# Separate step orders for the last four query groups, and the last output half scaled on ScalarE

## The chip, the cores and the metric

The kernel runs on one core of a Trainium2 chip. The metric is the device time of one execution in microseconds (us). The kernel before took 464.57 us, the median of 4 runs that lie between 464.2 and 465.14.

Engine names as the profile gives them: PE is TensorE's matmul, PEld its weight load, DVE is VectorE, ACT is ScalarE, POOL is GpSimd, and SP is SyncE, whose queue issues the transfers.

## What is computed

For each of 4 batches there are 12544 rows of q, k and v with 128 columns, and 49 agent rows. Two attentions are chained (agents over k and v, then q over agents), and the result goes through a feed-forward layer with three first matrices of which the largest product counts:

```python
agent_v = softmax(scale * agents @ k.T) @ v          # 49 x 128 per batch
x = softmax(scale * q @ agents.T) @ agent_v          # 12544 x 128 per batch
h = np.maximum(np.maximum(x @ w1, x @ w2), x @ w3)   # 768 wide
out = h @ w_out                                      # 50176 x 128, float32
```

## The kernel before, in words

The kernel never forms x. For each batch it multiplies agent_v into the differences w3-w1 and w2-w1 and into w1 @ w_out once, and keeps the result, 49 agents by 1792 columns, twice (in partitions 0 to 48 and 64 to 112) in a tile named G. After that a group of 1024 query rows needs only its exponentials and matmuls with G. Since max(w1, w2, w3) = w1 + max(w2 - w1, max(w3 - w1, 0)), the hidden layer is a relu, a max, and a linear part. The softmax's division comes last: the output is multiplied by the reciprocal of the sum of the exponentials.

The 50176 rows make 49 such groups, numbered 0 to 48. The k and v work of batches 1 to 3 is spread over earlier groups; the last dozen groups have none of it. A group s consists of these steps (the names are used throughout, as u2.48 for step u2 of group 48; f counts six slices of 128 of the 768 hidden columns):

| step | engine, line | work |
|---|---|---|
| s | PE L504 | 2 matmuls: q times agents |
| ex | ACT L510 | exponential, gives e_q |
| sum, rec | PE L518, DVE L524 | 4 small matmuls, then the reciprocals of the sums |
| u0 to u5 | PE L530 | 2 matmuls of 49 rows, on two halves of the array side by side: slice f of the (w3-w1) product |
| a0 to a5 | ACT L545 (a3: L542) | relu of u; a3 writes back into the same PSUM tile |
| v0 to v5 | PE L530 | 2 matmuls: slice f of the (w2-w1) product; v3 adds onto a3's tile |
| x0 to x5 | DVE L555 (x3: ACT L553) | max of v and a, gives r |
| lin0, lin1 | PE L560 | 2 matmuls that open an output half (4 of 8 blocks of 128 rows) with the linear part |
| oc00 to oc05, oc10 to oc15 | PE L569 | 4 matmuls: slice f of r times w_out onto output half 0 or 1 |
| sc0, sc1 | DVE L576 | output half times the reciprocals, PSUM to SBUF |
| store | SP L583 | one transfer of 512 KB to HBM, after sc0 and sc1 |

Three rings of buffers bind the steps: `uv` (3 PSUM pairs of banks, taken by u and v, freed by a, x), `om` (2 PSUM banks, taken by s, the sums' tile, lin0 and lin1; an output half is freed by its sc), and a_sb (3 tiles in SBUF, from a to x).

The order of the work is written out by hand. Each step gets a key, 6 times its group's number plus an entry of a table that `table(s)` at L101 picks (KEY, LATE, BORDER, BEGIN), and `emit` at L125 sorts all steps by key. A step whose needs or whose ring buffer are not yet met by steps already placed is put aside and goes in as soon as they are. So a table's entry only says where a step wants to stand; one far too early means "as soon as it can". The placed list, cut by engine, is each engine's program order, and engines run in order and wait for each other by semaphores. `put` (L588) sets needs: ex needs s; u needs ex; x needs v and a; oc needs its lin and x; sc needs rec and six oc. `out_scale` at L572 is the step sc. Before the change the last groups, like all from 36 on, use LATE.

Of the kernel before, what the change touches and what calls it, by code (L numbers as in the profile page):

```python
# [11 lines left out]
AF = mybir.ActivationFunctionType  # L12
# [4 lines left out]
def kernel(  # L17
# [18 lines left out]
    nc = tc.nc  # L36
    B, N, C = q.shape
    A = agents.shape[1]
    Dff = moe_w1.shape[1]
    scale = 1.0 / math.sqrt(C)  # L40
# [8 lines left out]
    NQ = B * NT // GT  # L49
# [46 lines left out]
        "oc11": 11.381, "oc13": 11.497,  # L96
    }
    PRODUCT_KEYS = (-8.717, -1.818)
    BEHIND = 2.6

    def table(s):  # L101
        if s + 1 in tails:
            return BORDER
        return BEGIN if s in tails and s < SB else KEY if s < SB else LATE
# [14 lines left out]
    def at(key, fn, name=None, needs=(), ring=None, frees=()):  # L119

        ops.append((key, len(ops), fn, name, needs, ring, frees))
# [140 lines left out]
    def k_group(b, t0, n, key, s):  # L264

        d = {}
        early = s is None
        K = None if early else table(s)
        if s == 0:
            key += BEHIND  # L270

# [109 lines left out]
    def k_tail(b, sum_key, keys, s):  # L381
# [46 lines left out]
        if s is not None:  # L428
            at(6.0 * (s - 1) + table(s - 1)["ke"] + 1.51, reduce, ("sum_e", b), [("kx", s - 1)])
            at(sum_key + 0.8, total, ("total", s), [("sum_e", b), ("ho", s)])  # L430
# [20 lines left out]
    def q_group(s):  # L451
# [4 lines left out]
        d = {}  # L456
# [28 lines left out]
        def evacuate():  # L485
# [4 lines left out]
            if not s:  # L490
                nc.scalar.activation(qT[:, :half], d["qT_ps"][:, :half], AF.Copy)  # L491

        K = table(s)
        q_dma = s >= SB or s + 1 in tails

# [76 lines left out]
        def out_scale(o):  # L572
            if "out" not in d:
                d["out"] = work.tile([P, GT, C], FP32, tag="o_sb", bufs=3, name="o_sb")
            j, m = 2 * pairs[o][0], 2 * len(pairs[o])
            nc.vector.tensor_tensor(  # L576
                out=d["out"][:, j:j + m, :],
                in0=d["o", o].rearrange("p (j c) -> p j c", c=C),
                in1=d["r"][:, j:j + m].unsqueeze(2).to_broadcast([P, m, C]), op=ALU.mult)
# [8 lines left out]
        def put(name, fn, *needs, ring=None, frees=()):  # L588
            at(key + K[name] + (BEHIND if s == 0 and name in ("sum", "rec") else 0), fn, (name, s), needs,
               ring, frees)  # L590
# [42 lines left out]
        for o in range(2):  # L633
            put(f"lin{o}", lambda o=o: out_linear(o), ("ex", s), *new_linear, ring="om",
                frees=[(f"sc{o}", s)])
            for f in range(NF):
                put(f"oc{o}{f}", lambda o=o, f=f: out_hidden(o, f), (f"lin{o}", s), (f"x{f}", s))
            put(f"sc{o}", lambda o=o: out_scale(o), ("rec", s),
                *[(f"oc{o}{f}", s) for f in range(NF)], *([("store", s - 3)] if s >= 3 else []))
# [36 lines left out]
    for b in range(1, B):  # L676
        for g in range(NK):
            s = (b - 1) * NT // GT + g
            hosting.add(s)
            k_group(b, g * KT, min(KT, NT - g * KT), 6.0 * s, s)  # L680
    for s, b in tails.items():
        assert s - 1 not in hosting
        k_tail(b, 6.0 * (s - 1) + table(s - 1)["ho"] + 0.001, [6.0 * s + PRODUCT_KEYS[i] for i in range(2)], s - 1)
    for s in range(NQ):
# [35 lines left out]
```

The softmax here doesn't subtract the row's maximum and nothing guards it: scores larger than these inputs give would overflow.

## Time and profile before

| what | value |
|---|---|
| median of 4 runs | 464.57 us |
| profiled execution, its own time | 465.01 us |
| its span, first to last instruction | 463.2 us |
| granted TensorE clock | 0.999 |
| period of one of the last groups (L542 of groups 46 to 48 starts at 433.50, 441.37 and 449.23) | 7.86 us |
| end of the last DVE instruction | 459.19 us |

The span is what the times inside the profile add up to; the execution's own time is 1.81 us longer. Times below are us from the span's start. The share of busy time says little here, because the matmuls' ends are modelled; what is read is which step started right after which other. In the last groups a group's steps overlap with those of its two neighbours, so that one period of 7.86 us holds one of each step, but of different groups.

### The profile page before, as it was taken

The numbers are of one execution on the slowest core, as the hardware profiler recorded it, in microseconds if no ns is written. First come the engines' busy times: TensorE is split into PE (matmuls) and PEld (weight loads), VectorE is DVE, ScalarE is ACT, GpSimd is POOL, SyncE is SP. The second block draws the span as 40 slices with busy tenths as digits, with TensorE's granted clock in tenths as the row PEclk, the third lists the DMA queues.
The fourth block names the chain that finished last, engine by engine and source line by source line (L and its number), as shares of the span: only waits on it lengthen the run. The fifth ranks groups of instructions, "written<-read, shape, count | busy, mean of one in ns | idle before, by whom it ended". The sixth has DMA issues, their size and how long they took to land.

```text
span 463.2 us, 13350 instructions
## 1 busy us (share of the span) xinstructions
PE 438.1 (95%) x5473; PEld 274.3 (59%) x5473; DVE 403.0 (87%) x512; ACT 396.2 (86%) x460; POOL 171.7 (37%) x179
## 2 busy tenths in 40 slices
PE   2597899999999999999999999999999999999995
PEld 2465466666665666666656666666656555555554
DVE  3255899999988999999989999999988999999995
ACT  3365889989899899899999998998999999999991
POOL 2244963553452545536272446353240101000000
PEclk9999999999999999999999999999999999999999
DMA  8999999996999899997998999996766586644122
GB/s 312 409 410 392 409 347 327 347 332 144 309 304 315 286 250 319 326 275 237 299 321 257 284 320 294 292 260 192 173 137 180 141 190 155 173 125 123 61 93 92
DMA packets 81450, 118.26 MB, mean 255 GB/s; under 512 B 55208, under 2 KB 56684, under 8 KB 81388
## 3 DMA queue, kind: packets, MB, share of 16 engines
q1 hardware_dynamic: 81184, 117.30, 83.2%
q8 instruction: 43, 0.70, 0.6%
q14 instruction: 20, 0.16, 0.1%
q10 hardware_dynamic: 203, 0.10, 0.1%
HBM read 78.74 MB, written 25.69 MB: 225 GB/s over the span
## 4 chain that ended last, share of the span: by engine, by line
PE 80%; DMA 8%; DVE 5%; ACT 4%; issue 1%; SPq 0%; POOL 0%; DVEq 0%; ACTq 0%
PE uv_ps L530 34%; PE o_ps L569 29%; PE o_ps L560 6%; DMA st<-in_k_dram 5%; PE m_ps L483 4%; DVE r L555 4%; PE m_ps L504 3%; ACT a_sb L545 2%; DMA st<-in_q_dram 2%; DMA st<-in_v_dram 2%; PE m_ps L323 2%; PE m_ps L312 1%; PE m_ps L518 1%; DVE o_sb L576 1%; ACT e_q L510 0%
## 5 line engine op out<-in xcount | busy, mean ns | idle before, releaser
L555 DVE TENSOR_TENSOR r<-uv_ps,a_sb 128x1024 bf16<-128x1024 f32 x245 | 297.1, 1220 | 14.7 <-PE uv_ps L530 6.5
L545 ACT ACTIVATE a_sb<-uv_ps 128x1024 bf16<-128x1024 f32 x245 | 240.8, 1026 | 14.9 <-PE uv_ps L530 13.6
L530 PE MATMUL uv_ps<-e_q,G 49*128 49x512 bf16 (+3 forms) x1248 | 187.2, 368 | 2.5 <-ACT uv_ps L542 0.7
L569 PE MATMUL o_ps<-wo_bf,r 128*128 128x128 bf16 x2352 | 175.3, 220 | 0.2 <-DVE r L555 0.2
L569 PEld LDWEIGHTS <-r 128*128 128x128 bf16 x2352 | 137.8, 98 | 40.1 <-issue 38.2
L530 PEld LDWEIGHTS <-G 49*128 49x128 bf16 x1248 | 57.7, 93 | 65.3 <-issue 33.3
L342 POOL TENSOR_TENSOR Eacc<-Eacc,e_k 128x441 f32<-128x441 f32 (+1 forms) x30 | 30.5, 1016 | 129.0 <-ACT e_k L317 129.0
L576 DVE TENSOR_TENSOR o_sb<-o_ps,recips 128x512 f32<-128x512 f32 x98 | 67.5, 689 | 9.2 <-PE o_ps L569 6.3
L478 POOL CAST q_bf<-st 128x1024 bf16<-128x1024 f32 x49 | 51.0, 1042 | 60.7 <-DMA qT<-q_bf 59.4
L553 ACT ACTIVATE r<-uv_ps 128x1024 bf16<-128x1024 f32 x49 | 50.2, 1024 | 18.0 <-PE uv_ps L530 17.7
L280 POOL CAST k_bf<-st 128x1152 bf16<-128x1152 f32 (+2 forms) x45 | 50.6, 1124 | 28.0 <-DMA st<-in_k_dram 24.7
L542 ACT ACTIVATE uv_ps<-uv_ps 128x1024 f32<-128x1024 f32 x49 | 49.6, 1012 | 1.6 <-issue 1.3
L560 PE MATMUL o_ps<-G,e_q 128*128 128x256 bf16 x196 | 38.0, 276 | 0.3 <-DVE o_sb L576 0.3
L287 POOL CAST v_bf<-st 128x1152 bf16<-128x1152 f32 (+1 forms) x33 | 37.5, 1136 | 0.6 <-PE m_ps L504 0.3
L510 ACT ACTIVATE e_q<-m_ps 128x512 bf16<-128x512 f32 x49 | 29.8, 608 | 0.5 <-PE m_ps L504 0.5
L300 DVE COPY kT<-uv_ps 128x1152 bf16<-128x1152 bf16 (+1 forms) x15 | 10.7, 713 | 16.8 <-PE uv_ps L294 16.8
L285 ACT ACTIVATE v_bf<-st 128x1152 bf16<-128x1152 f32 (+1 forms) x12 | 12.9, 1072 | 13.7 <-DMA st<-in_v_dram 13.6
L560 PEld LDWEIGHTS <-e_q 128*128 128x128 bf16 x196 | 12.5, 97 | 19.0 <-issue 17.8
L489 DVE COPY qT<-m_ps 128x1024 bf16<-128x1024 bf16 (+1 forms) x33 | 22.2, 673 | 0.8 <-PE m_ps L483 0.8
L483 PEld LDWEIGHTS <-q_bf 128*128 128x128 bf16 x264 | 14.9, 98 | 13.2 <-issue 10.6
L483 PE MATMUL m_ps<-ident,q_bf 128*128 128x128 bf16 x264 | 20.4, 220 | 0.5 <-POOL q_bf L478 0.5
L504 PE MATMUL m_ps<-qT,agT 128*64 128x512 bf16 (+3 forms) x104 | 19.9, 388 | 0.5 <-ACT qT L491 0.5
(71 smaller groups left out, 227.2 us busy)
## 6 DMA issues: line engine op xcount, KB each, us to landing
st<-in_q_dram SPq DMA_DIRECT2D x46, 512.0 KB, 4.9
out_dram<-o_sb SPq DMA_DIRECT2D x46, 512.0 KB, 3.1
st<-in_k_dram SPq DMA_DIRECT2D x40, 576.0 KB, 6.3
st<-in_v_dram SPq DMA_DIRECT2D x40, 576.0 KB, 7.7
st<-in_k_dram SPq DMA_DIRECT2D x3, 512.0 KB, 7.2
st<-in_v_dram SPq DMA_DIRECT2D x3, 512.0 KB, 7.9
wst<-in_moe_w_dram SPq DMA_DIRECT2D x3, 384.0 KB, 10.5
st<-in_q_dram SPq DMA_DIRECT2D x2, 384.0 KB, 4.8
```

Of the source, the lines that this page charges most:

```text
L280: nc.gpsimd.tensor_copy(out=d["kb"][:, :n, :], in_=d["k"][:, :n, :])
L287: nc.gpsimd.tensor_copy(out=d["vb"][:, :n, :], in_=d["v"][:, :n, :])
L478: nc.gpsimd.tensor_copy(out=d["qb"], in_=d["q"])
L483: nc.tensor.transpose(t[:, j * P:(j + 1) * P], d["qb"][:, j, :], ident)
L530: nc.tensor.matmul(t[:, h, j0 * P:j1 * P], G[b][h * H:h * H + A, col + f * P:col + (f + 1) * P], d["e"][h * H:h * H + A, j0 * P:j1 * P], s ...
L542: nc.scalar.activation(u, u, AF.Relu)
L545: nc.scalar.activation(a_sb[f], u, AF.Relu)
L553: nc.scalar.activation(r, v_ps[f], AF.Relu)
L555: nc.vector.tensor_tensor(out=r, in0=v_ps[f], in1=a_sb[f], op=ALU.max)
L560: nc.tensor.matmul(t[:, i * 2 * C:(i + 1) * 2 * C], d["e"][:, jj * P:(jj + 1) * P], G[batch[jj]][:, C1O:C1O + 2 * C], start=(i == 0), stop ...
L569: nc.tensor.matmul(t[:, c:c + C], r_sb[f][:, h, jj * P:(jj + 1) * P], wo_bf[:, f, :], start=False, stop=True, skip_group_check=True)
L576: nc.vector.tensor_tensor(out=d["out"][:, j:j + m, :], in0=d["o", o].rearrange("p (j c) -> p j c", c=C), in1=d["r"][:, j:j + m].unsqueeze( ...
```

## The change

There is a new list LAST of four tables, one each for groups 45 to 48, with a key for each step, and `table(s)` returns these for them. The last group's sc1 is done by four ScalarE instructions of 128x128, one per block of rows with its own column of reciprocals as scale, in place of one DVE instruction of 128x512.

```diff
+    LAST = [
+        {"v3": -164.4181, "x5": -156.2085, "oc14": -101.5261, "sc0": -56.4089, "a4": -33.1221,
...
+        {"a4": -135.5952, "s": -3.6850, "ex": -2.2030, "ho": -1.9346, "u0": -1.3390,
+         "sum": -0.9715, "a0": 0.1977, "rec": 0.3166, "u1": 1.4697, "u2": 3.5883, "v1": 3.7970,
+         "a1": 3.8096, "u3": 3.9647, "a2": 5.0765, "a3": 5.2628, "x1": 6.1940, "v0": 6.2913,
+         "v2": 6.3762, "v3": 6.7820, "x0": 10.4629, "sc1": 11.0558, "x3": 12.8641, "u4": 13.1350,
+         "v4": 13.7666, "x2": 16.1146, "u5": 19.9425, "v5": 20.9765, "sc0": 27.0577,
+         "x4": 27.8299, "oc04": 43.1860, "a5": 44.1320, "oc15": 44.9180, "lin1": 46.2961,
+         "oc13": 49.5958, "oc11": 49.9320, "oc12": 50.9170, "oc10": 55.9318, "oc14": 57.5404,
+         "oc05": 60.1508, "lin0": 70.3912, "oc03": 74.0752, "oc00": 92.6315, "oc01": 97.6449,
+         "x5": 102.3830, "oc02": 107.1067},
+    ]
     BEHIND = 2.6
 
     def table(s):
+        if s >= NQ - len(LAST):
+            return LAST[s - NQ]
         if s + 1 in tails:
             return BORDER
         return BEGIN if s in tails and s < SB else KEY if s < SB else LATE
...
             j, m = 2 * pairs[o][0], 2 * len(pairs[o])
+            if s == NQ - 1 and o == 1:
+
+                for i in range(m):
+                    nc.scalar.activation(d["out"][:, j + i, :], d["o", o][:, i * C:(i + 1) * C], AF.Copy,
+                                         scale=d["r"][:, j + i:j + i + 1])
+                return
             nc.vector.tensor_tensor(
```

What the keys come to, as program order (the steps of the tail; up to v5.47 the orders of PE differ in which slice's oc stands where, where sum stands, and in the places that the prediction names):

```
PE before:  v5.47 u1.48 oc04.46 oc05.46 u2.48 oc03.46 v0.48 u3.48 lin1.47 oc10.47 oc14.47
            v2.48 v3.48 v1.48 oc15.47 oc13.47 oc12.47 oc11.47 u4.48 u5.48 lin0.47 oc02.47 v4.48
            oc01.47 oc00.47 v5.48 oc04.47 oc05.47 oc03.47 lin1.48 oc10.48 oc14.48 oc15.48 oc13.48
            oc12.48 oc11.48 lin0.48 oc02.48 oc01.48 oc00.48 oc04.48 oc05.48 oc03.48
PE after:   v5.47 u1.48 oc03.46 oc05.46 oc00.46 u2.48 v1.48 u3.48 lin1.47 oc15.47 oc10.47 oc12.47
            oc14.47 v0.48 v2.48 v3.48 oc11.47 oc13.47 lin0.47 oc03.47 oc02.47 u4.48 v4.48
            oc00.47 oc05.47 oc01.47 u5.48 v5.48 oc04.47 lin1.48 oc13.48 oc11.48 oc12.48 oc10.48
            oc14.48 lin0.48 oc04.48 oc03.48 oc00.48 oc01.48 oc15.48 oc05.48 oc02.48
DVE before: x4.47 rec.48 x5.47 sc0.46 x0.48 x2.48 x1.48 sc1.47 x4.48 x5.48 sc0.47 sc1.48 sc0.48
DVE after:  x4.47 rec.48 x5.47 sc0.46 x1.48 x0.48 x2.48 sc1.47 x4.48 sc0.47 x5.48 sc0.48
ACT before: a4.47 a5.47 a0.48 a1.48 a2.48 a3.48 x3.48 a4.48 a5.48
ACT after:  a4.47 a5.47 a0.48 a1.48 a2.48 a3.48 x3.48 a4.48 a5.48 sc1.48 (four instructions)
```

The orders of SP and POOL are the same in both.

## The prediction, made before the changed kernel ran

> **What bounds the kernel now.** I read the page first (its chain of waits), then the timeline of each engine over the last 40 us, then the chain over the last 14 us. The page's chain says that the end hangs on PE, not on transfers:
>
> ```profile
> span 463.2 us, 13350 instructions
> PE 80%; DMA 8%; DVE 5%; ACT 4%; issue 1%; SPq 0%; POOL 0%; DVEq 0%; ACTq 0%
> ```
>
> But the last groups run in a loop of PE and DVE. In one period of DVE's timeline the reader is to see three pieces without a gap after a wait for PE:
>
> ```profile
> 442.73 2.35 DVE L555 TENSOR_TENSOR r<-uv_ps,a_sb 128x1024 bf16<-128x1024 f32 x2 [0.22 <-PE uv_ps L530]
> 445.00 0.68 DVE L576 TENSOR_TENSOR o_sb<-o_ps,recips 128x512 f32<-128x512 f32 x1
> 445.64 1.22 DVE L555 TENSOR_TENSOR r<-uv_ps,a_sb 128x1024 bf16<-128x1024 f32 x1
> ```
>
> These are x2.47 and x1.47, sc1.46, x4.47. u1.48 takes x4.47's buffer and starts at 446.91, 0.05 after it. From u1 to the next group's v2, PE never stops: 3.18 us, by the group before (439.05 to 442.23). So the loop is v2 to x2 0.50, x2 and x1 2.27, sc1 0.64, x4 and hand-over 1.27, PE 3.18: 7.86 us, the period. Both engines have slack outside it.
>
> The end is another stage. The chain of the last 5 us:
>
> ```profile
> 454.56 1.23 DVE r L555
> 455.79 0.05 issue
> 455.83 1.07 PE o_ps L569 x16
> 456.90 0.22 PE o_ps L560 x2
> 457.12 1.35 PE o_ps L569 x24
> 458.47 0.02 issue
> 458.50 0.69 DVE o_sb L576
> ```
>
> After x5.48, the last max, PE still has 42 matmuls, and the last scaling follows alone. The sums by stretch show the same (PE's count is the third column, DVE's the fifth); the last is the store:
>
> ```profile
> 449.23:455.78 6.55, 6.24 (x76) 4.10 (x73) 6.36 (x8) 3.98 (x5) 0.00 (x0) 1.00 0.20 80
> 455.78:459.19 3.41, 2.63 (x42) 2.43 (x42) 1.98 (x3) 0.00 (x0) 0.00 (x0) 1.00 0.41 159
> 459.19:463.20 4.01, 0.00 (x0) 0.00 (x0) 0.00 (x0) 0.00 (x0) 0.00 (x0) 0.87 0.33 131
> ```
>
> **Step sizes.** From PE's starts: an oc step (4 matmuls) is 0.225 (six take 1.35), lin 0.23, a u or v step before another 0.215; going from u/v to the full array or back makes a step 0.325 (0.32 to 0.33). DVE, start to next start: x 1.14, sc 0.63; 1.22 and 0.69 to their ends. ACT: a or x3 0.96 to the next, 1.02 to the end. From end to start: v to x on an idle DVE 0.11, u to a 0.04, v3 to x3 0.09, a buffer to PE 0.05, oc to sc 0.04. A u, v or oc step lasts 0.39 from its start to its end.
>
> **Groups 45 to 47: nothing.** No matmul is added. In the stretch from u1 to v2 other slices' oc stand, in the same number, and all their r tiles are ready; the DVE part has the same four steps. So I cost these orders at nothing; the loop covers them. Four edits depend on that cover.
> - u0.45 no longer follows v4.44 directly: oc01.43 stands between. That costs two array switches (0.22), but u0 waited 0.15 there for a4, so v5 is 0.08 later; and u1 after it waits 0.2 for x4. Without that slack the cost would be 0.08.
> - u5.46 moves behind lin0.45 and oc05.45, and waits with v4 for x1.46 (437.22), as v4 did. a5 still finds ACT busy with a4. Zero; without cover two steps, 0.45.
> - rec.45 and rec.46 move behind x5. Their sc0 comes 0.3 after DVE is free. Zero.
> - ex.45, ex.46 and ex.48 move behind x3. Behind ex wait lin0 (for its PSUM bank) and a4. With the trace's numbers of that period: v3.45 ends 427.11, so x3 runs from 427.20, ex from 428.16 and ends 428.76; lin0.44 starts at 428.82. It just fits, as the 0.48 for which ACT idled before a4 now lies before x3. No row shows ex behind x3, so bounds for lin0's delay: 0 (this sum; no gain, as ex was early before), and 0.17 a group (no overlap of x3 and ex, 0.06, and a hand-over as slow as the slowest in the chain, 0.12 ahead of a3.48). I take 0, the sum that uses the rows of this same engine back to back; three times 0.17 is for the range.
>
> **Group 48's order.** I follow the new program order from u1.48 (446.91, still tied to x4.47).
> - PE: oc03, oc05, oc00 of 46; u2.48 at 448.01. v1.48 needs x5.47's buffer (448.21): 448.26. u3 448.48, lin1.47 448.79, four oc, v0 450.02, v2 450.24. v3 needs a3: a2 starts when u2 ends, 448.44, a3 449.40, ends 450.42; v3 450.47. Then oc11, oc13, lin0, oc03, oc02 of 47, u4 452.02, v4 452.24, three oc, u5 453.34, v5 453.56, oc04.47 453.88, lin1.48 454.11.
> - DVE: sc0.46 finds its oc00 done (448.08) and starts at 448.13, not 448.55. x1.48 448.76 to 449.98. x0 has to wait for v0's end (450.41): 450.52; x2 451.66; sc1.47 452.80; x4 needs a4.48, which runs 452.45 to 453.48: 453.55 to 454.77; sc0.47 454.69; x5 455.32 to 456.54.
> - PE again: five oc of half 1 (oc14 at 455.24, after x4), lin0.48 455.46 (sc0.47 frees its bank at 455.37), four oc of half 0 to 456.59. oc15.48 wants 456.59, when x5 has just ended: no wait. oc05, oc02 456.82 and 457.04, ending 457.43.
>
> So PE issues its last step at 457.04, where the trace of before has it at 458.07 (oc03.48): 1.03 earlier. It is made of the stops of before, v3.48's wait for a3 (0.54 after v2 where 0.215 would do: 0.32) and oc15.48's for x5 (0.59 where 0.225 would do: 0.36), and of array switches: 13 from u1.48 on before, 9 after, four at 0.11; together 1.1, less some 0.05 that PE waits anew at v1 and v3. Nearly the whole gain is therefore PE's; the price is that DVE's x0.48 now stops 0.6 for v0.
>
> **The scaling.** sc0.48 on DVE: 457.47 to 458.16. sc1.48 on ACT follows oc15 (ends 456.98). No row shows a 128x128 scaling by a column from PSUM. Near rows, from the groups by shape:
>
> ```profile
> L240 ACT ACTIVATE wall<-o_ps 128x128 bf16<-128x128 f32 x1 | 0.3, 271 | 0.0
> L425 ACT ACTIVATE G<-uv_ps,r_ag 128x1024 bf16<-128x1024 f32 x3 | 3.3, 1115 | 0.0
> L545 ACT ACTIVATE a_sb<-uv_ps 128x1024 bf16<-128x1024 f32 x245 | 240.8, 1026 | 14.9 <-PE uv_ps L530 13.6
> ```
>
> 271 ns for the shape, and 1115 - 1026 = 89 ns for a column as scale: 0.36 each. The instruction behind such a one starts 1.01 after it (138.72, 139.73 in ACT's timeline), an overlap of 0.10. So four take 3 x 0.26 + 0.36 = 1.14; bounds 1.1 and 1.44 (no overlap). I take 1.14, from the row that has a column too: 457.02 to 458.16, beside sc0. The Trainium skill's page "ScalarE: Activation LUTs", section "Rules for kernel authors", gives plain multiplies to VectorE and not to ScalarE, which speaks against this edit. By the rows it is right for one half: 0.69 on DVE against 1.14. Followed here, DVE would do sc1 at 457.02 and sc0 from 457.65 to 458.34; with ScalarE the end is 458.16. The rule loses 0.18 here, only because DVE has the other half to do; at ScalarE's upper bound, 458.46, it would win by 0.12. So this edit is worth about 0.2 at best, not the 0.63 that it takes from DVE.
>
> sc1's first instruction also waits for transfers: its output buffer was last read by group 45's store, issued near 441.4 with 2.6 to 3.2 us to landing. Nothing is queued behind it on ACT, and the store waits for it and sc0. SP and POOL keep their order.
>
> **The sum.** 459.19 becomes 458.16: 1.03 us. The store and the end keep their 4.01 us, as the same 512 KB go after both halves. Span 462.17, execution 465.01 - 1.03 = 463.98. The runs' median lies 0.44 below that execution: 464.57 - 1.03 = 463.5 us. What a measurement of this kernel can tell from no change is about 0.2%, here 0.93 us; the forecast lies just beyond that line.
>
> **Rivals.**
> - The walk holds (chance 0.70): 463.5, own range 463.1 to 464.1.
> - The last group is starved more than the walk has it (0.24). For: x5.48's end and oc15, sc0.47 and lin0.48, a4 and x4 meet within 0.1 us, and any delay ahead of v0.48 goes through five DVE steps to the end. Against: each size is from this trace. With 0.65 lost on this path: 464.2.
> - Slower (0.06): ex behind x3. A delay d of lin0 goes straight into v4, x4 and u1, that is into the loop, in three groups. It cancels the gain at d = 0.34 and makes the kernel slower by 0.2% from d = 0.65; at 0.7 it gives 464.57 - 1.03 + 2.1 = 465.6. Against: the rows bound d at 0.17.
>
> **Numbers.** Range 463.0 to 464.7: it takes in ScalarE's upper bound (+0.3), the three delays of 0.17, the starved case, and below it the spread of the store's landing (2.6 to 3.2); it leaves out the slower case. Faster by over 0.2%: two thirds of the first case and a little of the second, 0.49; within: 0.45; slower: 0.06.
>
> **What would show it.** In the profile after: the period up to group 47 unchanged, u1.48 near 446.9; lin0.44 and lin0.46 without a wait for ex; PE's last step, oc02.48, starting near 457.0 with few gaps; DVE with one wait of about 0.6 before x0.48; four ScalarE rows of about 360 ns, 1.14 in all, ending within 0.2 of sc0.48. It is wrong if u1.48 is later than 447.1, if oc15 waits for x5, or if ScalarE's part is over 1.5 us.

## The result, and the profile after

The changed kernel takes 463.62 us (median of 34 runs, 463.19 to 464.95) against 464.81 for the kernel before (52 runs, 464.20 to 465.91). The ratio is 0.9977 with a 95% interval of 0.9972 to 0.9981: 1.07 us faster (0.88 to 1.30); the two medians lie 1.19 apart. The forecast was 463.5, a gain of 1.03, counted from the 464.57 of the first four runs.

The profiled execution took 463.82 us, with a span of 461.7. Line numbers in its rows are the old ones plus 40, from `out_scale`'s scaling on plus 46; L619 is new. The page hides the change (PE has 81% of its chain where it had 80%): shares of a 462 us span cannot show 1 us. The chain of the last microseconds does (start, length, engine, tile, line, number of instructions):

```profile
454.35 1.12 PE o_ps L609 x20
455.47 0.22 PE o_ps L600 x2
455.69 1.13 PE o_ps L609 x20
456.82 0.02 issue
456.84 0.37 ACT o_sb L619
```

There is no wait for DVE in it any more, and nearly no "issue" (time in which an engine waited for nothing that the profile shows) before the last scaling: PE goes from one step to the next. Before, the same place held a whole max (1.23 us of DVE) and 42 matmuls behind it. DVE's own timeline shows where the last max stands now, and ACT's row the new scaling:

```profile
454.51 0.68 DVE L622 TENSOR_TENSOR o_sb<-o_ps,recips 128x512 f32<-128x512 f32 x1
455.11 1.21 DVE L595 TENSOR_TENSOR r<-uv_ps,a_sb 128x1024 bf16<-128x1024 f32 x1
457.29 0.69 DVE L622 TENSOR_TENSOR o_sb<-o_ps,recips 128x512 f32<-128x512 f32 x1 [0.96 <-PE o_ps L609]
```
```profile
456.84 1.14 ACT L619 ACTIVATE o_sb<-o_ps,recips 128x128 f32<-128x128 f32 x4 [2.19 <-PE o_ps L609]
```

These are sc0.47, x5.48 and sc0.48, and the four instructions of sc1.48. x5.48 now ends at 456.32, 0.54 later than before, and still the last scalings end at 457.98, 1.21 earlier. Both halves end in the same hundredth. Of the 1.21, 0.11 is no part of the change: this trace runs about that much earlier from well before the changed groups on (a3 of group 41 starts at 394.06, before at 394.19; u1.48 at 446.80, before 446.91). From u1.48 to the end of the last scaling it is 11.18 us, before 12.28: 1.10 gained.

The stretches of the end, in the same columns as before (stretch, length, busy time and count of PE, PEld, DVE, ACT, POOL, clock, transfers):

```profile
447.00:455.00 8.00, 8.00 (x103) 5.71 (x102) 7.46 (x8) 6.21 (x7) 0.00 (x0) 1.00 0.18 70
...
458.00:461.70 3.70, 0.00 (x0) 0.00 (x0) 0.00 (x0) 0.00 (x0) 0.00 (x0) 1.00 0.35 142
```

PE is busy 8.00 of 8.00 us. In the stretch where the old trace had 6.24 of 6.55 busy, with 76 matmuls, this one (449.12 to 455.67, 0.11 earlier) has 6.55 of 6.55 and 91 matmuls. The last stretch, store and end, is 3.70 us where before it was 4.01; the prediction had it unchanged.

### The profile page after: what moved, and what is told of

Its sections match the earlier page's. It is cut to its first block, busy times and chain, and to the rows that moved or that the text cites. A ratio compares the mean times of both kernels' runs of the same rounds, so it can differ in the third digit from the quotient of the medians.

```text
span 461.7 us, 13354 instructions
## 1 busy us (share of the span) xinstructions
PE 437.4 (95%) x5473; PEld 274.5 (59%) x5473; DVE 402.2 (87%) x511; ACT 397.2 (86%) x464; POOL 171.5 (37%) x179
## 4 chain that ended last, share of the span: by engine, by line
PE 81%; DMA 8%; DVE 4%; ACT 3%; issue 1%; SPq 0%; POOL 0%; ACTq 0%; DVEq 0%
PE uv_ps L570 34%; PE o_ps L609 30%; PE o_ps L600 6%; DMA st<-in_k_dram 5%; PE m_ps L523 4%; PE m_ps L544 3%; DVE r L595 3%; ACT a_sb L585 2%; DMA st<-in_q_dram 2%; DMA st<-in_v_dram 2%; PE m_ps L363 2%; PE m_ps L352 1%; PE m_ps L558 1%; DVE o_sb L622 0%; ACT e_q L550 0%
```

## The experiments

The same early step lies up to 0.5 us apart in two traces, so places in different kernels are compared after lining them up at a DVE step that both have in the same place (sc0.46 with the new orders, x4.48 with the old).

**The scaling alone.** The four ScalarE instructions of the diff, put into the kernel before.

> The kernel before with only the scaling moved: group 48's sc1 as four ScalarE instructions, old orders. Theory (the gain is PE's, from group 48's order): sc1.48 is not on the path there, since it starts at 456.94 with 1.5 us to spare before sc0.48 at 458.50, so 0.0 us against before (within 0.1). Rival (the gain is the 0.63 us that DVE no longer does): about 0.6 us faster than before.

Measured: ratio 1.0003 (0.9995 to 1.0011), no difference. What DVE no longer does was not on the path.

**The orders alone.** The new tables without the lines in `out_scale`.

> The changed kernel with sc1.48 back on DVE as one instruction: new orders alone. Theory: DVE does sc1 and then sc0 after the last matmuls, 0.63 + 0.69 from oc15's end, so 0.18 us slower than the changed kernel, about 0.9 us faster than before. Rival (the scaling is half of the change): 0.5 us slower than the changed kernel or more.

Measured: 463.44 us, ratio 0.9970 (0.9959 to 0.9982). In time it cannot be told from the full change. In its profile DVE does both scalings at the end,

```profile
456.68 1.29 DVE L616 TENSOR_TENSOR o_sb<-o_ps,recips 128x512 f32<-128x512 f32 x2 [0.52 <-PE o_ps L609]
```

and ends at 457.97, with sc0.46 0.15 earlier than in the changed kernel: lined up 0.14 later than with ScalarE (expected 0.18). So nearly the whole gain is the orders', and the new scaling is worth 0.14 in the trace and too little for the runs to show.

**Two tables of four.** A miss, and an instructive one.

```diff
-        if s >= NQ - len(LAST):
+        if s >= NQ - 2:
```

> The changed kernel with new tables for groups 47 and 48 only; 45 and 46 keep the old one. Three oc steps of group 46 then stand earlier than in the changed kernel, where PE waits for x4. Theory (the loop covers the orders of groups 45 and 46, and v1.48 waits for x5.47 at the same time): the same time as the changed kernel within 0.15 us, about 1.1 us faster than before. Rival (each of the four tables brings a part): half of the gain or less.

Measured: 466.23 us, ratio 1.0033 (1.0022 to 1.0044), slower than before by 1.5 us. The waits from 430 us on (who waited for whom: us in total, times, longest), first of the changed kernel, then of this one:

```profile
DVE r L595 <- PE uv_ps L570: 0.9, 3, 0.5
```
```profile
DVE r L595 <- PE uv_ps L570: 3.2, 5, 1.0
...
ACT e_q L550 <- PE m_ps L544: 1.0, 1, 1.0
```

The keys of neighbouring groups share one scale. With group 47 on its new table and 46 on the old one, s.47 came to stand behind v1.46, 1.0 us later, ex.47 waited for it, and the loop from u1.47 to u1.48 grew from 7.86 to 8.50 us. So this kernel did not test what it was made for; it says that an order in these groups can cost much, not that the new one gains there. The next two do it with explicit lists.

**Old up to u1.48, then new; and new up to u1.48, then old.** Each step that a list names gets its place from the list, all others keep the key of their table:

```diff
+        step = f"{name[0]}.{name[1]}" if isinstance(name, tuple) else None
+        if step in TAIL:
+            key = 1000 + TAIL.index(step)
         ops.append((key, len(ops), fn, name, needs, ring, frees))
```

> The order of before, step for step, up to u1.48, and from u1.48 on the order of the changed kernel, written as an explicit list (the three steps of oc0 of group 46 that stand behind u1.48 are the same number, of the slices that the old order has left); sc1.48 on ScalarE. Theory (the whole gain is made after u1.48): the changed kernel's time within 0.15 us, some 1.1 us faster than before. Rival (the orders of groups 45 to 47 bring part of it): at most 0.7 us faster.

> The counterpart: the order of the changed kernel up to u1.48, and from there the order of before; sc1.48 on ScalarE as in the changed kernel. Theory: the time of before within 0.15 us. Rival (orders of groups 45 to 47 matter): 0.4 us faster or more.

Measured: 463.34 us, ratio 0.9969 (0.9957 to 0.9980), the whole gain, for the first; 464.76 us, ratio 1.0001 (0.9993 to 1.0009), none of it, for the second. The chain of the first has the end of the changed kernel, without a wait (28 matmuls: seven oc steps), then that of the second, which ends as the old kernel's did:

```profile
455.46 1.58 PE o_ps L579 x28
```
```profile
454.75 1.22 DVE r L605
455.98 0.05 issue
456.02 1.07 PE o_ps L619 x16
```

The three tables' work on groups 45 to 47 neither gains nor costs: the runs say so to within 0.4 us, and in the traces the way from a3 of group 41 to a3 of group 48 is 55.04 us in the second kernel (394.38 to 449.42) and in the kernel before (394.19 to 449.23).

**ex behind x3, twelve times.** In the kernel before, in the table LATE:

```diff
-        "s": -4.972, "ex": -4.712,
+        "s": -4.972, "ex": -4.000,
```

> The kernel before with one entry of the late table changed, so that ex stands behind x3 in 12 groups (37 to 48) instead of in none. Each delay d of lin0 would count 12 times. Theory: d is 0 to 0.05, so 0.0 to 0.6 us slower than before, and the period stays within 0.05 of 7.86. Rival (ex behind x3 delays lin0 by the row-based upper bound of 0.17 or more): 2 us slower or more, period 8.03 or more.

Measured: 464.65 us, ratio 0.9992 (0.9984 to 1.0000). ACT's timeline of one period, behind the row of the kernel before that shows its gap:

```profile
428.71 4.90 ACT L545 ACTIVATE a_sb<-uv_ps 128x1024 bf16<-128x1024 f32 x5 [0.48 <-PE uv_ps L530]
```
```profile
419.21 1.02 ACT L553 ACTIVATE r<-uv_ps 128x1024 bf16<-128x1024 f32 x1 [0.55 <-PE uv_ps L530]
420.13 0.59 ACT L510 ACTIVATE e_q<-m_ps 128x512 bf16<-128x512 f32 x1
420.71 4.90 ACT L545 ACTIVATE a_sb<-uv_ps 128x1024 bf16<-128x1024 f32 x5
```

ACT's gap has moved from behind x3 to in front of it, and a4 follows ex at once. The period is 7.86 us (a3 starts at 417.64 and at 425.50), as before, and all twelve groups have ex behind x3. So no delay d shows, and the slower rival falls.

**Four array switches more.** Two entries of the changed tables, oc04 of group 47 and v4 of group 48 (the rest of their lines is left out):

```diff
-         "oc04": 48.8226, ...
+         "oc04": 26.5100, ...
...
-         "v4": 13.7666, ...
+         "v4": 17.0000, ...
```

> The changed kernel with v4.48 put behind oc00.47 and v5.48 behind oc04.47, so that PE changes between the 49-row steps and the full array four times more and no step's need becomes late. Theory (after u1.48 PE never waits and a switch costs 0.11 us): 0.44 us slower than the changed kernel, PE's last step at 457.3 where the changed kernel has it at 456.86. Rival (the end hangs on DVE's chain to x5.48, PE has slack): no slower, since x5 does not move.

Measured: 464.08 us, ratio 0.9987 (0.9981 to 0.9994), 0.46 slower than the changed kernel, by the two ratios. Its chain:

```profile
451.81 0.32 PE uv_ps L570 x2
452.14 0.33 PE o_ps L609 x4
452.47 0.32 PE uv_ps L570 x2
452.79 0.55 PE o_ps L609 x8
```

Each step that stands alone between two of the other kind is 0.32 to 0.33 instead of 0.22. x5.48 moved by nothing (454.98 to 456.19 with the origin 0.13 earlier), and the end came 0.42 later: PE sets it, and a switch costs about 0.11 (0.42 / 4).

**The last max's matmuls earlier.** In the changed table of group 48, oc15 gets the key 49.7 and x5 49.69, so that x5's matmuls come early while DVE's order stays.

> The changed kernel with oc15.48 moved up to the second oc of its half, with oc05 third in its own half; x5.48 stays where it is on DVE. Theory (the place of the matmuls that need the last max decides the end): PE stops at oc15 until x5 ends at about 456.3, then has 11 steps of 0.22 left, ends its last step's start near 458.8: about 1.9 us slower than the changed kernel, 0.9 slower than before. Rival (the gain came from fewer array switches alone): within 0.2 us of the changed kernel.

Measured: 465.32 us, ratio 1.0017 (1.0010 to 1.0023): 0.8 slower than before (0.9 expected), with all the saved switches in it. The chain shows the old picture, and behind these lines come 26 matmuls more (24 of half 0's and lin0's two) and sc0 from 458.88:

```profile
454.72 1.23 DVE r L595
455.95 0.05 issue
456.00 1.29 PE o_ps L609 x20
```

**One step of the old order moved.** In the old order oc15.48 goes behind oc11.48.

> The kernel before with one step moved: oc15.48, the first step that waits for x5.48, stands behind oc13, oc12 and oc11 of its half instead of ahead of them. Theory (oc15's wait of 0.36 us for x5 is one of the three parts of the gain and can be had alone): 0.3 us faster than before, since PE fills the wait and lin0.48 is then met by its bank's release at 456.4. Rival (DVE's chain sets the end): no change.

Measured: 464.37 us, ratio 0.9993 (0.9984 to 1.0001): not settled by time. In the trace the last scaling ends at 458.76, with x4.48 0.11 earlier: 0.32 gained of the 0.30 expected, and the wait is gone (24 matmuls in one piece):

```profile
455.06 1.34 PE o_ps L576 x24
456.40 0.29 PE o_ps L567 x2
```

**A version meant to be faster.** Since PE has no gap left from u1.48 on, the place to look is what follows its last step. The edits are named in the expectation; the core is a store for each half:

```diff
-        at(key + 12.2, store, ("store", s), [("sc0", s), ("sc1", s)])
+        if s == NQ - 1:
+            for o, name in ((1, "store1"), (0, "store")):
+                at(key + 12.2, lambda o=o: store(o), (name, s), [(f"sc{o}", s)])
+        else:
+            at(key + 12.2, store, ("store", s), [("sc0", s), ("sc1", s)])
```

> Made to be faster than the changed kernel: the same order up to u5.48; then x5.48 ahead of sc0.47 on DVE, sc0.47 on ScalarE (idle there), output half 0 of group 48 in a free buffer of the uv ring so that it need not wait for sc0.47, oc15.48 four steps earlier, half 1 scaled by DVE and stored at once by a transfer of its own of 256 KB, half 0 scaled by DVE (three blocks) and ScalarE (one), then the second transfer. Theory (PE's last step cannot come earlier, only what follows it): PE's last step at 456.9 as in the changed kernel, last scaling done 0.1 earlier, and 0.6 less of store as half the bytes are left: 0.7 us faster than the changed kernel, 1.8 faster than before. Rival (the store's time is all latency, not bytes): 0.1 faster than the changed kernel.

Measured: 463.28 us, ratio 0.9966 (0.9954 to 0.9978). The store's part came out (from the last scaling to the end 2.99 us instead of 3.70), the scaling's did not: DVE's part of half 0 began only when ScalarE's block of the same PSUM tile had ended. The ratios lie 0.0011 apart, 0.5 us ahead of the changed kernel where 0.7 was expected, with overlapping intervals.

```profile
457.81 0.56 DVE L635 TENSOR_TENSOR o_sb<-uv_ps,recips 128x384 f32<-128x384 f32 x1 [0.60 <-ACT o_sb L626]
```

> As the split store, but half 0 of group 48 is scaled by DVE alone in one instruction, since there DVE's three blocks began only when ScalarE's one had ended (457.81 in place of 457.43). Theory: sc0 starts right after PE's last step and ends 0.25 earlier than in the split store; store and end stay at 3.0 us: 0.7 us faster than the changed kernel on the same chip, 0.25 faster than the split store. Rival (ScalarE's block was not what DVE waited for): as the split store, 0.4 faster than the changed kernel.

> The changed kernel itself once more, on the same chip as the kernel above, for a comparison side by side: 1.1 to 1.4 us faster than before.

Measured on one chip: 463.00 us, ratio 0.9970 (0.9958 to 0.9981), for the mended version, and 463.96 us, ratio 0.9978 (0.9972 to 0.9985), for the changed kernel. The sequence is as meant: sc0 starts 0.20 after the end of sc1, without ScalarE in it, and the landing times of its last three stores are 2.7 us for group 47's 512 KB and 2.0 for each half:

```profile
457.06 0.69 DVE L632 TENSOR_TENSOR o_sb<-uv_ps,recips 128x512 f32<-128x512 f32 x1 [0.20 <-PE uv_ps L617]
```
```profile
DMA to landing us min/median/max: 2.0/2.0/2.7
```

The spans of the two profiled executions are 460.8 and 461.9 us. The intervals of the two ratios overlap, and of its eleven executions seven lie below the changed kernel's median and four above, so that this version beats the changed kernel is likely and not shown. Nor do the runs decide between the 0.7 expected and the rival's 0.4. It is faster than the kernel before.

## Why the prediction was right, point by point

- **The loop covers groups 45 to 47.** Right, by the two mixed orders. The four edits that depended on cover cost nothing taken together: from a3 of group 41 to u1.48 it is 52.74 us, before 52.72. Of the four, only ex behind x3 was tried by itself.
- **Group 48's walk.** From u1.48 the prediction's step-by-step count (the walk) had PE's last step 10.13 us later and the trace has 10.06. x5.48 was to end 9.63 after u1.48 and ends 9.52 after it. DVE's stop for v0.48, counted from x1's end, is 0.46 (the walk: 0.54). oc15 does not wait. The closest meeting is there: oc15 starts 0.10 behind x5's end.
- **The three sources of the gain.** The switches are shown by experiment (0.42 in the trace for four). oc15's wait is shown in the trace of the single move (0.32, with 0.36 as the wait itself). The third, v3.48's wait for a3 (0.32), was not tried by itself; it is about what is left of the 1.10, and the new trace has v3 0.21 after v2. The chain of before waits for a3 there, the new one goes through v0, v2 and v3 in one piece:

```profile
449.23 1.03 ACT uv_ps L542
...
450.29 0.61 PE uv_ps L530 x4
```
```profile
449.98 0.75 PE uv_ps L570 x6
```

- **The scaling.** 1.14 us for four instructions, to the hundredth what the row with a column and its overlap gave; both halves end together. Its worth of 0.2 at best came out as 0.14 in the trace. The rule that the prediction cites (the Trainium skill's page "ScalarE: Activation LUTs", section "Rules for kernel authors": multiplies to VectorE) was right about the engine: 0.69 on DVE for the half that takes ScalarE 1.14. Overruling it here paid in the trace, as DVE had the other half to do, and in nothing that the time shows.
- **Store and end.** Here a step failed: "The store and the end keep their 4.01 us". In the profiled pair they took 4.04 (459.19 to 463.23, the span's end to the hundredth) and 3.70. So the pair's spans differ by 1.10 + 0.34 + 0.11 = 1.55 us, more than the 1.07 of the times. The spans that are on record for each execution show why both can be so. In the comparison on one chip, the median span falls by 1.3 us, from 463.1 (32 executions of the kernel before) to 461.8 (21 of the changed one), but what an execution takes beyond its span rises in the median from 1.78 to 1.98 us. In the changed kernel's 34 executions of the first comparison the medians are 461.5 and 2.06. This time beyond the span is over 2.3 us in 15 of these 55 executions and in none of the kernel before's 128 in the experiments' comparisons, whose median span is 463.0. The prediction kept it fixed too, when it took the gain off the execution's 465.01. Two terms that it held constant thus moved against each other, the store and end down by 0.2 to 0.4 (the span's 1.3 to 1.5 less 1.10), the time beyond the span up by 0.2 to 0.3. That 1.03 met 1.07 so closely is in part luck; that the part before the store came out as 1.10 is not. Why the time beyond the span is longer no trace shows, and it stays open: in six executions each of the orders alone and of old then new its median is 1.82.
- **The starved and the slower rival** both fell, the first because the walk's close meetings held, the second by the twelvefold test.

## What to carry to other kernels

At the end of a kernel ask which work can only start after the last slow step, and put everything else in front of it: in the old order, moving one step of four matmuls behind three others took a 0.3 us wait away in the trace, and in the changed kernel, moving the same step forward cost 1.7 us. Where a tuned loop is bound by a dependency through two engines, reorder only outside the loop, and test by splicing whole orders, not by mixing tables whose keys were set against each other. An instruction taken off a busy engine gains nothing if its place was not on the path.

## What the runs showed of the hardware that was not expected

In the profiled pair the last store and the end are faster after the change by about 0.3 us, though the bytes are the same. The queues' transfers in the last microseconds (packets, MB, share of the 16 transfer engines), first of the kernel before (455 to 464 us), then of the changed one (454 to 462):

```profile
q1 hardware_dynamic: 288, 1.05, 29.6%
q8 instruction: 1, 0.02, 0.6%
```
```profile
q1 hardware_dynamic: 288, 1.05, 32.6%
```

In the kernel before one transfer of instructions shares the transfer engines with the last stores, and the two stores land after 3.1 us in the median instead of 2.6. In the profiled executions of all four kernels with the old end (before, scaling alone, ex behind x3, new then old) that transfer of 16 KB starts between 457.4 and 459.1, and from the last scaling to the end they take 3.96 to 4.23 us. In the eight other profiles with one last store it comes after the end, ends before the store has begun, or is not in the record, and they take 3.67 to 3.71; one of them has the old order but for one step (3.67), so the order as such does not make the difference. That it is the cause was not tried, and how often it happens in the executions of which only the time and the span are known is open.

Not expected either: two engines reading different columns of one PSUM tile did not overlap, in a program in which DVE's instruction waits for ScalarE's (0.38 us lost in the split store); with the halves in different PSUM tiles, as in the changed kernel, they ran side by side (457.29 to 457.98), though both wrote to one output tile. So the shared PSUM tile is the likely reason; that alone was not varied.
